# The last 2048 tokens through Strassen's scheme in two blocks, and the low parts of q, k and v on GpSimd

## The chip, the core and the metric

The kernel runs on one core of a Trainium2 chip. The metric is device time in microseconds (us) of one execution; before the change the median of three runs was 1136.08 us (1135.66 to 1136.82). The engines are called as in the profile: PE is TensorE (PEld its weight loads), DVE is VectorE, ACT is ScalarE, POOL is GpSimd, and SP is SyncE, whose queue issues nearly all DMAs.

## The reference

Causal attention with a decay of cumulated logarithms, for 8 batches of 8 heads, 576 tokens, 64 dimensions; then a feed-forward network (FFN) with softplus on all 4608 tokens:

```python
scores = np.matmul(q, k.transpose(0, 1, 3, 2)) / np.sqrt(D)
cum = np.cumsum(np.log(np.clip(f, 0.0001, 1.0)), axis=-1)
scores = np.where(causal, -1e9, scores + cum[:, :, :, None] - cum[:, :, None, :])
attn = softmax(scores, axis=-1)
x = np.matmul(attn, v)                     # tokens x 512 after the heads are joined
h = x @ w_in                               # 4608 x 512 @ 512 x 2048
g = np.maximum(h, 0.0) + np.log1p(np.exp(-np.abs(h)))
out = g @ w_out                            # 4608 x 2048 @ 2048 x 512
```

All is float32. The kernel keeps the precision by splitting a factor into a high and a low part of a narrower type (suffixes h and l) and multiplying three times: high by high, high by low, low by high.

## The kernel before

**Attention.** Batch 0 is treated apart, in plain float32. Batches 1 to 7 are 56 jobs of one head each. A job computes scores in six pieces (L859 and L860, 12 matmuls; the piece of 64 columns marks one job's start in a trace), the row minimum with the mask on DVE (L864), the exponential on ACT (L903), the division by the row sum (L933) on ACT, POOL or DVE, turns the weights on PE (L996, 15 short matmuls a job), splits them into ph and pl, multiplies with the split v (L1143, 10 matmuls), and adds two parts into x (L1193). So 37 PE instructions a job are attention.

**The operands of the scores.** q and k of a job lie in a tile T, of which there are two, used in turn: job n + 2 takes the tile of job n. `prepare` fills it when the last score of job n has been read: the high part (L227, T from raw), the low part `l_` (L811, on DVE), and four moves by DMA from one half of the partitions to the other (L814): one after the high part, one after the low part, one after that move, and one after both. The first score of job n + 2 waits for the last move. v has a high part and a low part `vl` (L785, on DVE).

**FFN.** Tokens 0 to 511 go in two plain blocks and one of 256; tokens 512 to 3583 in six wide blocks of 512. For each of 16 chunks of 128 of the 2048 middle columns, a wide block takes 12 matmuls of 512 columns up (L1336) and, for four tiles of 128 tokens, 12 down (L1423): 384 in a block. Between lies the gate, three passes on ACT (L1369, L1372, L1375), one on DVE (L1383), and the split of g (L1391). Half of a block's down products come at its end, as a tail, from parts of g kept in DRAM. A block starts when the attention of its last token is done, and its matmuls are dealt out among the steps of the following jobs.

**Strassen.** The last 1024 tokens (`super_block`, one of them) wait until all attention is issued. Even and odd tokens, two halves of the 512 inputs and pairs of chunks make 2 by 2 blocks; Winograd's form of Strassen's scheme takes seven products in place of eight. For each of eight pairs of chunks that is 7 x 6 matmuls up (L1856); down is as before, 12 for each chunk (L1978). POOL adds blocks of the weights (L1738), DVE adds products (L1885), and `lay_x` makes the sums of x (L1648) and splits them (L1678).

**The order.** Python lists all steps, and a planner with costs (`Plan.run`) sets each engine's order by when it expects a step's inputs and buffers to be there. Engines then run their lists and wait by semaphores. `on` in `add` names the engines that a step may go to, with a cost, a bias and a mark for steps that share a port of the memory.

Of the kernel before, what the change touches and what calls it, by code (L numbers as in the profile page):

```python
# [31 lines left out]
FFN_RANK = 0  # L32
SHORT = 512
SUPER, NSUPER = 1024, 1
BEHIND = 190
# [7 lines left out]
class Op:  # L43
# [4 lines left out]
    def __init__(self, on, emit, after, takes, lag):  # L48
        self.on = on if isinstance(on, list) else [on]
        self.emit, self.after, self.takes, self.lag = emit, list(after), takes, lag  # L50
        self.users = []
        self.missing = len(self.after)


class Plan:
# [33 lines left out]
    def start_of(self, op, clock):  # L89
# [4 lines left out]
        for tag in set(op.takes):  # L94
            n, free = op.takes.count(tag), self.free[tag]
            early = self.queue[tag][0] is not op
            if len(free) < n + early or (early and not op.loose):
                return None
# [132 lines left out]
def tile_decay_attention_softplus_ffn(  # L231
# [113 lines left out]
    g_d = dpool.tile([2, NFC, P, TB], F32, name="g_d")  # L345
    odd_d = dpool.tile([NSUPER, 2, NFC, P, SUPER // 2], F32, name="odd_d")
# [316 lines left out]
    def attention(job):  # L663
# [114 lines left out]
        def split_v():  # L778
# [11 lines left out]
            vl = add(subs(nv * D), v_lo, after=[vh])  # L790
# [3 lines left out]
        def prepare():  # L794
# [29 lines left out]
            l_ = add(On("DVE", 0.75, 0.0, True), lo, after=[h_])  # L824
# [8 lines left out]
        def stat_tile(ti, into=None):  # L833
# [12 lines left out]
            for i, (a, z, acc) in enumerate(pieces):  # L846
# [31 lines left out]
                else:  # L878
                    o = add(on, scores, after=st["T"], takes=("att",), loose=True)
                if quad:  # L880
# [340 lines left out]
    splits = {}  # L1221
# [29 lines left out]
    def ffn_block(i):  # L1251
# [11 lines left out]

        def split_x():
            if plain:
                st["split"] = [d for a, z, d, _ in wrote[0] if a < t0 + nt and z > t0]
                return
            ready, low, at = [], [], t0
            while at < t0 + nt:
# [25 lines left out]
                if lo + w == S:  # L1295
                    give("x32", splits[b])
                at += w
            st["split"], st["low"] = ready, low
# [249 lines left out]
    def super_blocks():  # L1548
# [66 lines left out]
        spots = [(x, j) for x in OPERANDS for j in range(2)]  # L1615
# [5 lines left out]
        def lay_x(t0):  # L1621

            done, reads, pieces = {}, {}, []
            pos = t0
            while pos < t0 + SUPER:
                b, lo = pos // S, pos % S
                w = min(t0 + SUPER - pos, S - lo)
                pieces.append((b, lo, w, slice((pos - t0) // 2, (pos - t0 + w) // 2)))
                pos += w

            WHERE = dict(B11=(0, 0), B12=(0, 1), B21=(2, 0), B22=(2, 1))

            for j in range(2):
                room = {}

                def less(x, one, other, j=j, room=room):

                    if x not in room:
                        box = {}

                        def begin(e, box=box):
                            box["x"] = buf("fe", [P, 512], f"late_{x}{t0}_{j}")

                        room[x] = box, add(NO_ENGINE, begin, takes=("fe",), lag=0.0), [], []
                    box, begun, made, _ = room[x]

                    def go(e, a, b, c):
                        e.tensor_sub(box["x"][:, c], a(), b())  # L1648

                    for i, (b, lo, w, c) in enumerate(pieces):  # L1650
                        (a1, n1), (a2, n2) = (value(v, i) for v in (one, other))
                        o = add(
                            [subs(w // 2), On("POOL", 0.2 + w * 0.0011, 0.0, True)], lambda e, a1=a1, a2=a2, c=c: go(e, a1, a2, c),
                            after=n1 + n2 + [begun],
                        )
                        made.append(o)
                        for v in (one, other):
                            (room[v][3] if v in room else reads.setdefault(b, [])).append(o)

                def value(x, i, j=j, room=room):  # L1660
# [532 lines left out]
    for n in range(len(jobs) + 1):  # L2193
# [56 lines left out]
        if n >= nstart:  # L2250
            while splits_left:
                splits_left.pop(0)()
# [54 lines left out]
```

## Time and profile before

| | |
|---|---|
| median of three runs | 1136.08 us |
| the profiled execution, its own time | 1137.25 us |
| its span, first to last instruction | 1135.4 us |
| TensorE clock granted over the span | 0.999 (2.4 GHz all the way) |
| busy share of PE, DVE, ACT, POOL | 99%, 75%, 74%, 16% |

The span falls into batch 0 and the weights (to about 114 us), the 56 jobs with the FFN between them (to 950 us), and Strassen's block with the last tails (to the end). PE counts as busy from an instruction's start to its modelled end, and these overlap; how fast it works is read from the distance of starts.

### The profile page before, as it was taken

Reading aid. Unit: us, or ns where it says so; the run is one execution under the profiler, and the core shown is the slowest. Engines: PE = TensorE matmul, PEld = TensorE weight load, DVE = VectorE, ACT = ScalarE, POOL = GpSimd, SP = SyncE. Lnnn points to the kernel's source line nnn. Section 1 sums busy time; section 2 is a strip of 40 time slices with the busy share of each in tenths; the row PEclk is TensorE's granted clock in tenths of the full one; section 3 lists DMA queues with packets and bytes.
Section 4 is the critical chain, followed back from the end, with each engine's and each line's share of the span. In section 5 each row is a group of like instructions: output and inputs, shape, how many; then the busy total and the mean of one; then the engine's idle time right before and its main releaser. Section 6 shows DMA issues by size and latency. Waiting matters only on the chain.

```text
span 1135.4 us, 19910 instructions
## 1 busy us (share of the span) xinstructions
PE 1123.0 (99%) x6230; PEld 939.8 (83%) x6230; DVE 850.8 (75%) x2131; ACT 838.8 (74%) x2033; POOL 185.6 (16%) x225
## 2 busy tenths in 40 slices
PE   9999999999999999999999999999999999999998
PEld 7766789888888888888888888888888888888887
DVE  7888999987787777777777778677867778867610
ACT  6888798889877777678767787677867875766610
POOL 3323221111111001000010000000000013555200
PEclk9999999999999999999999999999999999999999
DMA  8868676566575656666576466665657535322481
GB/s 244 252 183 229 179 215 163 148 174 175 158 208 159 174 164 175 161 186 170 151 203 189 137 179 182 165 179 158 174 153 208 142 99 162 130 93 98 162 278 38
DMA packets 160489, 192.97 MB, mean 170 GB/s; under 512 B 54944, under 2 KB 120768, under 8 KB 160384
## 3 DMA queue, kind: packets, MB, share of 16 engines
q1 hardware_dynamic: 160216, 191.55, 59.1%
q8 instruction: 50, 0.82, 0.3%
q14 instruction: 55, 0.45, 0.1%
q10 hardware_dynamic: 168, 0.15, 0.0%
HBM read 114.17 MB, written 44.34 MB: 140 GB/s over the span
## 4 chain that ended last, share of the span: by engine, by line
PE 86%; DVE 8%; ACT 3%; DMA 2%; issue 1%; SPq 0%; DVEq 0%
PE acc L1423 24%; PE h L1336 24%; PE b L996 7%; PE o L1143 7%; PE late_E L1978 4%; PE s L860 4%; PE s L859 4%; PE late_A L1856 2%; PE late_D L1856 2%; PE late_C L1856 2%; DVE s L864 1%; PE late_B L1856 1%; PE late_D L1978 1%; PE late_C L1978 1%; PE late_A L1978 1%
## 5 line engine op out<-in xcount | busy, mean ns | idle before, releaser
L864 DVE CUSTOM_DVE_ANT_0 s<-s,cmask 128x288 f32<-128x288 f32 (+6 forms) x320 | 137.1, 440 | 60.6 <-PE s L860 54.2
L903 ACT ACTIVATE pb<-s,negm 128x288 f32<-128x288 f32 (+5 forms) x272 | 143.3, 531 | 45.8 <-DVE negm L864 43.9
L933 POOL TENSOR_SCALAR pb<-pb,rsum 128x448 f32<-128x448 f32 (+2 forms) x44 | 59.5, 1353 | 415.8 <-ACT e L1375 192.9
L1336 PE MATMUL h<-xh,wl 128*128 128x512 f32 (+1 forms) x448 | 126.0, 380 | 0.0
L1336 PE MATMUL h<-xh,wih 128*128 128x512 f32 (+1 forms) x448 | 117.0, 383 | 0.5 <-DVE gl L1391 0.5
L1018 DVE TENSOR_TENSOR pl<-b,ph 128x512 fp32r<-128x512 f32 x168 | 107.1, 662 | 9.5 <-ACT ph L227 8.7
L1336 PE MATMUL h<-xl,wih 128*128 128x512 f32 (+1 forms) x448 | 113.9, 376 | 0.0
L227 ACT CAST ph<-b 128x512 fp32r<-128x512 f32 (+2 forms) x169 | 80.1, 492 | 34.8 <-PE b L996 33.1
L859 PE MATMUL s<-T 128*128 128x192 f32 (+1 forms) x336 | 99.3, 304 | 3.0 <-ACT pb L903 1.3
L1423 PE MATMUL acc<-woh_dt_float32r,gh 128*128 128x512 f32 x248 | 99.2, 400 | 0.0
L1369 ACT ACTIVATE e<-h 128x512 f32<-128x512 f32 x112 | 66.8, 596 | 43.3 <-PE h L1336 42.2
L860 PE MATMUL s<-T 68*128 68x192 f32 (+1 forms) x336 | 98.2, 296 | 0.0
L1423 PE MATMUL acc<-woh_dt_float32r,gl 128*128 128x512 f32 x248 | 97.4, 393 | 0.0
L1423 PE MATMUL acc<-wol_dt_float32r,gh 128*128 128x512 f32 x248 | 97.1, 392 | 0.0
L1336 PEld LDWEIGHTS h<-xl,wih 128*128 128x128 f32 x448 | 80.8, 188 | 16.6
L1336 PEld LDWEIGHTS h<-xh,wl 128*128 128x128 f32 x448 | 80.1, 189 | 13.0 <-issue 0.5
L1383 DVE SCALAR_TENSOR_TENSOR h<-h,e 128x512 f32<-128x512 f32 x104 | 73.3, 705 | 20.4 <-ACT e L1375 19.4
L1336 PEld LDWEIGHTS h<-xh,wih 128*128 128x128 f32 x448 | 77.8, 189 | 11.8 <-DVE gl L1391 0.7
L1143 PE MATMUL o<-ph,vhl 128*128 128x512 f32 x336 | 84.8, 290 | 0.0
L1391 DVE TENSOR_TENSOR gl<-h,gh 128x512 fp32r<-128x512 f32 x104 | 71.5, 687 | 16.0 <-ACT gh L227 14.6
L996 PE MATMUL b<-halves,pb 128*128 128x128 f32 x512 | 82.2, 272 | 0.0
L1372 ACT ACTIVATE e<-e 128x512 f32<-128x512 f32 x112 | 70.8, 632 | 1.9
(368 smaller groups left out, 2812.9 us busy)
## 6 DMA issues: line engine op xcount, KB each, us to landing
T<-T SPq DMA_DIRECT2D x224, 144.0 KB
wl<-wil_d SPq DMA_DIRECT2D x56, 512.0 KB
raw<-in_qkT SPq DMA_DIRECT2D x112, 144.0 KB
g_d<-gh SPq DMA_DIRECT2D x84, 128.0 KB
g_d<-gl SPq DMA_DIRECT2D x84, 128.0 KB
vr<-in_vR SPq DMA_DIRECT2D x64, 160.0 KB
out<-ob SPq DMA_DIRECT2D x28, 256.0 KB
sto<-in_w_out SPq DMA_DIRECT2D x11, 512.0 KB
```

Source lines behind the costliest of these rows:

```text
L227: (e.tensor_copy if hasattr(e, "tensor_copy") else e.copy)(out, in_)
L859: e.matmul(o, qA[:, S - end : S - q0], kA[:, a:z], start=True, stop=False)
L860: e.matmul(o, qB[0:ST, S - end : S - q0], kB[0:ST, a:z], start=False, stop=True)
L864: e.tensor_tensor_reduce(out=box["o"], in0=box["o"], in1=cmask[0:n_q, right - w : right], scale=-0.125, scalar=m0 if i else 3.0e38, op0=AL ...
L903: e.activation(o, box["o"], AF.Exp, bias=m1, scale=-1.0, accum_out=acc)
L996: e.transpose(box["ps"][0 : x.shape[1], at : at + one.shape[1]], x, one)
L1018: e.tensor_sub(box["l"], box["ps"][:, 0:w], box["h"].bitcast(F32))
L1143: e.matmul(boxes[gi]["ps"][0:m, a:z], st["vhl"][:, c, 0:m], pbox[which][:, o : o + z - a], start=gi in fresh and which == "h", stop=gi == ...
L1336: e.matmul(o, l, r, start=m == 0, stop=m == 11)
L1423: e.matmul(st["acc", tt], l, r[fc], start=first and m == 0, stop=last and m == 2,)
L1856: e.matmul(banks[to], stationary(x, j), at(b, y, j), start=start and m == 0, stop=m == 5, skip_group_check=not start,)
L1978: e.matmul(banks[x], l, r[fc], start=first and m == 0, stop=final and m == 2)
```

## The change

`NSUPER` goes from 1 to 2: tokens 2560 to 4607 go through Strassen's scheme, in two blocks of 1024, after all attention; wide blocks are left for tokens 512 to 2559, four in place of six. T still has two tiles.

x of batches 1 to 7 is written to a tensor `x_d` in DRAM, four DMAs of 288 KB a batch, each when two heads are done. The wide blocks behind token 1152 and both Strassen blocks load x from there (1 MB a load), where before they read the tile that attention had written; a tile of x is free once it is stored.

The low parts `vl` and `l_` may go to POOL, with a bias that prefers it by 9 us.

The pacing of the FFN among the jobs has new constants, and a rule that saves matmuls of a block for later jobs. The first Strassen block's second half of odd outputs is accumulated in the banks of the even ones (E0, E1) and reads through the buffers gh and gl; its last eight steps are issued behind the second block's start.

```diff
-SUPER, NSUPER = 1024, 1
-BEHIND = 190
+SUPER, NSUPER = 1024, 2
+POOLB = -9.0
+BEHIND, FILL, REST, START = 190, 5, 4, 3
...
-            vl = add(subs(nv * D), v_lo, after=[vh])
+            vl = add([subs(nv * D), On("POOL", 0.2 + nv * D * 0.0022, POOLB, True)], v_lo, after=[vh])
...
-            l_ = add(On("DVE", 0.75, 0.0, True), lo, after=[h_])
+            l_ = add([On("DVE", 0.75, 0.0, True), On("POOL", 0.2 + S * 0.0022, POOLB, True)], lo, after=[h_])
...
+    def store_x(b, g):
+
+        def store(e):
+            e.dma_start(out=x_d[g, :, b * S : (b + 1) * S], in_=x_of[b][:, g, :])
+
+        need = [d for _, _, d, g_ in wrote[b] if g_ == g]
+        stores[b, g] = add_dma(store, 288, after=need)
...
+        def split_stored():
+            ready, low, box = [], [], {}
+
+            def load(e):
+                box["x"] = buf("x32", [P, NCC, S], f"xr{i}")[:, :, 0:nt]
+                e.dma_start(out=box["x"], in_=x_d[:, :, t0 : t0 + nt].rearrange("c p t -> p c t"))
...
+            if t0 + nt > 2 * S:
+                split_stored()
+                return
...
+                ld = add_dma(load, 1024, after=stored(t0, SUPER, (j, j + 2)), takes=("x32",))
...
-            two = tail(["C", "D"], 2 * P, s == NSUPER - 1)
+            end = s == NSUPER - 1
+            spots = [(x, j) for x in OPERANDS[: 7 if end else 2] for j in range(2)]
+            one = tail(["B", "A"], 0, spots, False)
+            two = tail(["E0", "E1"], 2 * P, spots, end)
...
-        share = sum(c for c, _ in ffn) / (until - n + 1 + DELAY) / max(1, len(units))
+        here = sum(c for c, _ in ffn)
+        share = here / (until - n + 1 + (START if n <= nstart + H else DELAY))
+        if n > nstart + H:
+            later = sum(NFC * on_pe(WIDE, 24).cost for x in ready_at.values() for _ in x)
+            share = min(share, (here + later) / (len(jobs) - n + REST))
+        share /= max(1, len(units))
...
-        plan.late, left = 0, []
-        for unit in units:
+        plan.late, left = 0, units[len(units) - 8 :]
+        for unit in units[: len(units) - 8]:
             unit()
+    for unit in left:
+        unit()
```

**PE.** Between the last scores of one job (s_4_288) and the first of the next (s_1_0) in the steady part stood 24 FFN matmuls (h, acc) and the ten of the values (o). Before, at the 37th job, the first half of them:

```order
L859 MATMUL s_4_288_7812<-T_1151 128x288
L860 MATMUL s_4_288_7812<-T_1151 128x288
L1423 MATMUL acc_0_7676<-woh_dt_float32r,gh_3_7717 128x512
L1423 MATMUL acc_0_7676<-wol_dt_float32r,gh_3_7717 128x512
L1423 MATMUL acc_0_7676<-woh_dt_float32r,gl_3_7722 128x512
L1423 MATMUL acc_1_7677<-woh_dt_float32r,gh_3_7717 128x512
L1423 MATMUL acc_1_7677<-wol_dt_float32r,gh_3_7717 128x512
L1423 MATMUL acc_1_7677<-woh_dt_float32r,gl_3_7722 128x512
L1336 MATMUL h_6_7829<-xh_6951,wih 128x512 x4
L1336 MATMUL h_6_7829<-xh_6951,wl_3_7639 128x512 x2
L1143 MATMUL o_1_7842<-ph_1_7749,vhl_7314 128x512
L1143 MATMUL o_1_7842<-pl_1_7755,vhl_7314 128x512
```

In the changed kernel at the 38th job, one of the closest places (L866 and L867 are the scores, L1151 the values, L1479 the down products):

```order
L866 MATMUL s_4_288_7322<-T_1370 128x288
L867 MATMUL s_4_288_7322<-T_1370 128x288
L1151 MATMUL o_1_7328<-ph_1_7293,vhl_6925 128x512
L1151 MATMUL o_1_7328<-pl_1_7305,vhl_6925 128x512
L1479 MATMUL acc_0_7026<-woh_dt_float32r,gh_4_7184 128x512
L1479 MATMUL acc_0_7026<-wol_dt_float32r,gh_4_7184 128x512
L1479 MATMUL acc_0_7026<-woh_dt_float32r,gl_4_7194 128x512
L1479 MATMUL acc_1_7027<-woh_dt_float32r,gh_4_7184 128x512
L1479 MATMUL acc_1_7027<-wol_dt_float32r,gh_4_7184 128x512
L1479 MATMUL acc_1_7027<-woh_dt_float32r,gl_4_7194 128x512
L1151 MATMUL o_1_7328<-ph_2_7302,vhl_6925 128x448
L1151 MATMUL o_0_7349<-ph_0_7291,vhl_6925 128x64
```

Behind these come six more values and then the next job's first score: six FFN matmuls stand there, where before 24 stood. Over the 47 jobs from the ninth to the last but one the changed order has 1479 FFN matmuls of 512 columns, 31.5 a job, and the order before 2178, or 46.3 a job.

**POOL.** In the steady part, POOL had the division of some weights (pb or p by rsum) alone, one or two a job:

```order
L933 TENSOR_SCALAR pb_93<-pb_93,rsum_87 128x448
L933 TENSOR_SCALAR p_92<-p_92,rsum_88 64x64
L933 TENSOR_SCALAR pb_94<-pb_94,rsum_88 128x320
L933 TENSOR_SCALAR p_91<-p_91,rsum_89 64x64
L933 TENSOR_SCALAR pb_93<-pb_93,rsum_89 128x320
```

In the changed kernel each job has two more there, the low part of v (L792) and that of q and k (L818):

```order
L792 TENSOR_TENSOR vhl_5364<-vr_5234,vhl_5364 128x6x64
L818 TENSOR_TENSOR T_1370<-raw_5193,T_1370 128x576
L941 TENSOR_SCALAR p_92<-p_92,rsum_90 64x64
L792 TENSOR_TENSOR vhl_5493<-vr_5405,vhl_5493 128x6x64
L818 TENSOR_TENSOR T_1137<-raw_5350,T_1137 128x576
L941 TENSOR_SCALAR p_91<-p_91,rsum_87 64x64
L792 TENSOR_TENSOR vhl_5651<-vr_5575,vhl_5651 128x6x64
L818 TENSOR_TENSOR T_1370<-raw_5484,T_1370 128x576
```

All 56 low parts of q and k and all 56 of v have moved from DVE to POOL, and T's moves now follow a POOL instruction that stands behind the low part of v.

**SP.** Stores of x stand in the queue that issues T's moves. In the changed kernel, about the 36th job:

```order
L777 DMA raw_6940<-in_qkT 64x9x64
L781 DMA raw_6940<-in_qkT 64x576
L719 DMA vr_6954<-in_vR 128x320
L724 DMA vr_6954<-in_vR 128x1x64
L1234 DMA x_d<-x_5_6743 128x576
L821 DMA T_1137<-T_1137 64x576
L1363 DMA wl_3_6990<-wil_d 128x1024
```

The store (L1234) has come in ahead of the last move (L821) of a tile T; before, such places held loads and the stores of g and of the output.

## Rows read from the trace of the kernel before

**Rows 1.** The page: busy time and share of the span, the span in 40 slices for some engines and the granted clock, and the shares by engine of the chain that ended last.

```profile
PE 1123.0 (99%) x6230; PEld 939.8 (83%) x6230; DVE 850.8 (75%) x2131; ACT 838.8 (74%) x2033; POOL 185.6 (16%) x225
...
PE   9999999999999999999999999999999999999998
...
DVE  7888999987787777777777778677867778867610
ACT  6888798889877777678767787677867875766610
...
PEclk9999999999999999999999999999999999999999
...
PE 86%; DVE 8%; ACT 3%; DMA 2%; issue 1%; SPq 0%; DVEq 0%
```

**Rows 2.** Timeline of PE near the end: start and duration of single matmuls of 512 columns, the first and the last of 36 in a row.

```profile
1085.15 0.39 PE L1978 MATMUL late_B<-woh_dt_float32r,late_T 128*128 128x512 f32 x1
1085.37 0.39 PE L1978 MATMUL late_B<-wol_dt_float32r,late_T 128*128 128x512 f32 x1
...
1093.08 0.39 PE L1978 MATMUL late_A<-woh_dt_float32r,late_T 128*128 128x512 f32 x1
```

**Rows 3.** Busy time by stretch: from:to and length in us, then PE, PEld, DVE, ACT and POOL busy (with the number of instructions), the granted clock, the DMA share and GB/s. The first holds seven jobs, the ninth to the fifteenth; the second six jobs of the steady part; the third the first eight jobs; the fourth runs from the last values to Strassen's first product; the fifth lies in Strassen's block.

```profile
211.98:304.20 92.22, 91.75 (x518) 78.36 (x517) 73.06 (x192) 80.92 (x206) 11.22 (x11) 1.00 0.58 159
594.18:693.85 99.67, 99.67 (x540) 84.82 (x539) 75.95 (x190) 78.18 (x188) 6.16 (x5) 1.00 0.58 163
114.00:211.98 97.98, 97.05 (x655) 81.48 (x656) 93.94 (x256) 85.24 (x229) 19.74 (x18) 1.00 0.69 188
950.15:962.44 12.29, 12.29 (x55) 10.14 (x55) 12.14 (x30) 5.28 (x14) 4.33 (x6) 1.00 0.63 198
990.00:1079.00 89.00, 89.00 (x394) 73.74 (x393) 61.05 (x109) 58.73 (x110) 38.12 (x51) 1.00 0.36 125
```

**Rows 4.** Groups of equal instructions in the first stretch of rows 3: the wide FFN matmuls and the score piece of 64 columns, one a job.

```profile
L1336 PE MATMUL h<-xh,wl 128*128 128x512 f32 x56 | 16.6, 395 | 0.0
L1336 PE MATMUL h<-xh,wih 128*128 128x512 f32 x56 | 15.6, 401 | 0.5 <-DVE gl L1391 0.5
L1336 PE MATMUL h<-xl,wih 128*128 128x512 f32 x56 | 15.1, 392 | 0.0
L1423 PE MATMUL acc<-woh_dt_float32r,gl 128*128 128x512 f32 x33 | 12.9, 392 | 0.0
L1423 PE MATMUL acc<-woh_dt_float32r,gh 128*128 128x512 f32 x32 | 12.8, 401 | 0.0
L1423 PE MATMUL acc<-wol_dt_float32r,gh 128*128 128x512 f32 x32 | 12.5, 391 | 0.0
...
L859 PE MATMUL s<-T 128*64 128x64 f32 x7 | 1.3, 193 | 0.0
```

**Rows 5.** Groups over the whole span: the low parts of q and k (L811) and of v (L785) on DVE, and on POOL the division of weights (L933) and two-input sums of 256 columns (L1738); busy us, mean ns of one, idle before.

```profile
L811 DVE TENSOR_TENSOR T<-raw,T 128x576 fp32r<-128x576 f32 x56 | 42.3, 755 | 0.2
L785 DVE TENSOR_TENSOR vhl<-vr,vhl 128x384 fp32r<-128x384 f32 x56 | 31.7, 565 | 1.2 <-ACT vhl L227 0.6
...
L933 POOL TENSOR_SCALAR pb<-pb,rsum 128x320 f32<-128x320 f32 x18 | 21.3, 1183 | 145.4 <-DVE rsum L917 71.6 <-DVE x L1193 37.4 <-ACT x L227 19.0
...
L1738 POOL TENSOR_TENSOR p<-p,p 128x256 f32<-128x256 f32 x16 | 12.0, 747 | 1.3
...
L933 POOL TENSOR_SCALAR pb<-pb,rsum 128x576 f32<-128x576 f32 x4 | 6.9, 1722 | 0.0
```

**Rows 6.** Timeline of one tile T in the dense part: the last score of its job, the high and low parts, the moves (L814; the last line holds the fourth and others), and the first score of the job after next.

```profile
194.50 0.30 PE L860 MATMUL s<-T 68*128 68x288 f32 x1
...
194.77 0.45 DVE L227 CAST T<-raw 128x576 fp32r<-128x576 f32 x1
...
195.50 1.32 SPq L814 DMA_DIRECT2D T<-T  x2
195.57 0.75 DVE L811 TENSOR_TENSOR T<-raw,T 128x576 fp32r<-128x576 f32 x1
...
199.57 0.51 SPq L814 DMA_DIRECT2D T<-T  x1
...
202.73 2.37 SPq L814 DMA_DIRECT2D T<-T  x3
...
207.14 0.25 PE L859 MATMUL s<-T 128*128 128x192 f32 x1
```

**Rows 7.** Waits of SP's queue over the whole span, by line: us in total, times, longest us.

```profile
SPq L1395 <- ACT gh L227: 85.0, 38, 5.1
...
SPq L814 <- DMA T<-T: 53.9, 50, 3.5
```

**Rows 8.** Timeline of POOL and DVE about a low part of v.

```profile
825.39 0.44 POOL L933 TENSOR_SCALAR p<-p,rsum 64x64 f32<-64x64 f32 x1 [9.14 <-PE s L860]
...
825.88 0.86 DVE L785 TENSOR_TENSOR vhl<-vr,vhl 128x384 fp32r<-128x384 f32 x1
```

**Rows 9.** Timeline of PE at the longest single wait of the steady part, in brackets.

```profile
450.78 0.33 PE L859 MATMUL s<-T 128*128 128x192 f32 x1 [0.94 <-ACT ph L227]
```

More of the change, by code (lines that the diff above doesn't have):

```diff
@@ L51, in __init__ @@
         self.users = []
+        self.end = self.guard = None
         self.missing = len(self.after)
@@ L95, in start_of @@
             n, free = op.takes.count(tag), self.free[tag]
-            early = self.queue[tag][0] is not op
+            head = self.queue[tag][0]
+            early = 0 if head is op else head.takes.count(tag) if EARLY else 1
             if len(free) < n + early or (early and not op.loose):
+                return None
+            if early and op.guard and op.guard.end is None:
                 return None
@@ L1218, in attention, with stored @@
         )
-    splits = {}
+    splits, stores = {}, {}
+    def store_x(b, g):
[3 more added lines that the diff above has]
+        stores[b, g] = add_dma(store, 288, after=need)
+        if b > 1 and g == NCC - 1:
+            give("x32", [add(NO_ENGINE, mark, after=[stores[b, c]]) for c in range(NCC)])
+    def stored(t0, n, planes=range(NCC)):
+        return [stores[b, g] for b in range(t0 // S, (t0 + n - 1) // S + 1) for g in planes]
     kept_read = {}
@@ L1294, in split_x @@
                 splits.setdefault(b, []).append(l_)
-                if lo + w == S:
-                    give("x32", splits[b])
                 at += w
+                if b == 0 and lo + w == S:
+                    give("x32", splits[0])
+                if b == 1 and at == t0 + nt:
+                    give("x32", splits[1] + [add(NO_ENGINE, mark, after=[stores[1, g]]) for g in range(NCC)])
             st["split"], st["low"] = ready, low
@@ L1621, in lay_x @@
         def lay_x(t0):
[L1623 to L1631, printed above, removed]
-            for j in range(2):
[L1634 to L1660, printed above, removed]
-                    b, lo, w, c = pieces[i]
@@ new lines, in value, with less, go @@
+                    return (lambda: xbox["x"][:, k, odd:SUPER:2]), [ld]
+                def less(x, one, other, j=j, room=room, reads=reads, value=value):
+                    box = {}
+                    (a1, n1), (a2, n2) = value(one), value(other)
+                    def go(e):
+                        box["x"] = buf("fe", [P, 512], f"late_{x}{t0}_{j}")
+                        e.tensor_sub(box["x"], a1(), a2())
+                    o = add(
+                        [subs(n), On("POOL", 0.2 + n * 0.0022, 0.0, True)], go, after=n1 + n2,
+                        takes=("fe",), loose=True,
+                    )
+                    room[x] = box, None, [o], []
+                    for v in (one, other):
+                        (room[v][3] if v in room else reads).append(o)
@@ L1701, in lay_x @@
                     give("fe", ops)
-            for b, ops in reads.items():
-                give("x32", splits.get(b, []) + ops)
+                give("x32", reads)
             return done
@@ L2036, in step @@
                     loads["used", fp].append(o)
+                    if not spots_of[fp] and tiles[-1] == k == 1:
+                        give("gh", [o])
+                        give("gl", [o])
                     return o
```

114 lines of the change are left out of this document (75 added, 39 removed).

## The prediction

> **What bounds the kernel now.** I read the page first. PE is busy for 99% of the span at the full clock of 2.4 GHz, and the chain that ended last is 86% PE; in 39 of the 40 slices PE is at nine tenths or more [rows 1]. Busy time of PE says little, since starts overlap, so the second view is the distance of starts: near the end 36 matmuls of 512 columns start between 1085.15 and 1093.08 us, which is 7.93 / 35 = 0.2266 us for one [rows 2]. That is the price of one FFN matmul wherever PE has all it needs.
>
> The third view is the table by stretch [rows 3]. In the steady part six jobs take 99.67 us with 540 PE instructions. A job has 37 of attention, so 540 - 222 = 318 are FFN matmuls (some counted at the edges): 318 x 0.2266 = 72.1 us, and (99.67 - 72.1) / 6 = 4.6 us of PE are left for a job's attention, waits included. In the dense part seven jobs take 92.22 us with 168 + 97 = 265 FFN matmuls [rows 4]: 60.0 us, and (92.22 - 60.0) / 7 = 4.6 us again. So a job costs 4.6 us and 0.2266 us for each FFN matmul beside it, at either density. PE's own work is the bound, and the first question is how many matmuls the change takes away.
>
> **The change part by part.** *Fewer matmuls up.* Two wide blocks took 2 x 16 x 12 = 384 up; Strassen's block takes 8 x 7 x 6 = 336. Down stays 384. That is 48 x 0.2266 = 10.9 us off PE's list, at the price of a place where PE never waits.
>
> *720 matmuls leave the attention part.* They go to a stage where PE, in the stretch of rows 3 that lies there, is busy 89.00 of 89.00 us, with DVE at 69% and ACT at 66% [rows 3], and a second block of the same steps has the same loads. Nothing is lost there.
>
> *The 56 jobs stand closer.* The changed order has 31.5 FFN matmuls a job where 46.3 stood, so a job should take 4.6 + 31.5 x 0.2266 = 11.7 us, against 4.6 + 46.3 x 0.2266 = 15.1. Whether ACT and DVE keep up is the open question. ACT: 80.92 / 7 = 11.6 us a job in the dense part at 37.9 FFN matmuls, and 78.18 / 6 = 13.0 us in the steady part at 53 [rows 3]; the line through these has 0.10 us a matmul, and gives 10.9 us at 31.5. DVE the same way: 10.4 and 12.7 us, 0.15 a matmul, 9.5 us at 31.5; from that go the two low parts, 0.755 + 0.565 = 1.3 us [rows 5], which leaves 8.2. Together 19.1 us on two engines that have 23.4: 82%. The dense part had 22.0 of 26.3, or 83%, and steps that may go to either engine can even it out. So the nearest row for the coming density is the dense part, where PE was busy 91.75 of 92.22 us, and a job cost no more than elsewhere. I take 0.5% of 47 x 11.7 = 550 us, 2.8 us, as lost to waits. From below: none. From above, by the first eight jobs, with DVE at 96%: 97.98 - 97.05 is 1% [rows 3], 5.5 us; and one wait of 0.94 us, the longest of the steady part [rows 9], shows what a single miss costs.
>
> *Low parts on POOL.* A two-input sum of 256 columns takes 0.747 us there; between 320 and 576 columns a division grows by 1.722 - 1.183 = 0.54 us, so 2.1 ns a column [rows 5]. Estimates from these: 1.4 us for 576 columns and 1.0 us for 384 (by plain proportion 1.7 and 1.1). POOL had 11.22 / 7 = 1.6 us a job in the dense part [rows 3], so some 4 of 11.7 us: far from full. DVE is relieved; but the low part of q and k is a link in T's cycle, which grows by 1.4 - 0.755 = 0.65 us. That costs nothing as long as T is ready before PE has run out of other work. In the dense part a cycle took 207.14 - 194.50 = 12.6 us from the last score to the first score of the job after next [rows 6], so 13.3 with POOL. Counted in the changed order, with the distances that the same instructions had before, PE has 13.4 us of work at the shortest between those two scores, 15.9 on the mean. So the cover is there, thin in some five jobs: 0 us, and 0.65 in each if it is gone, 3 us.
>
> The Trainium skill speaks against this move: GPSIMD Engine Reference, section 4.1, gives elementwise work to VectorE, GpSimd being about twice as slow for two inputs. The rows agree, 1.4 against 0.755 us; the sum would change only through the cycle of T, which is the last rival below. SBUF — State Buffer, section "Who interferes with whom", adds that a GpSimd instruction and a DVE instruction with two SBUF inputs shut each other out for a whole instruction. One row agrees: a low part of v that began while POOL worked took 0.86 us in place of 0.565 [rows 8].
>
> What is left on DVE of that kind is little once the low parts are gone; at 0.3 us for each of two POOL steps a job DVE would go from 8.2 to 8.8 us of 11.7. PE would not see it.
>
> *x through DRAM.* Four stores of 288 KB a batch in SP's queue, and seven loads of 1 MB. No row shows these; the nearest are the moves of T, 144 KB, whose landings SP waited for 50 times, 3.5 us at most [rows 7]. Before a block's first products that adds a store and a load, perhaps 10 us. The changed order keeps a wide block's tail, over 60 matmuls, for two jobs there, some 23 us of PE work, so I cost it at nothing; uncovered, three times 5 us. A store that waits in SP's queue holds back the moves of T behind it; waits of one kind there reach 5.1 us already [rows 7]. This too would come out as a longer cycle of T.
>
> *The joints.* Before, 54 matmuls covered the way from the last values to the first Strassen product, 12.29 us without a gap [rows 3]; now 66 do. Between the blocks the changed order mixes the last steps of one with the first products of the other. 0 us, at most 2. *The start* (to 114 us) is ordered anew in small ways: 0, with 3 us to either side; DVE, at 96% in the first eight jobs, is relieved there, which could give 2 us back.
>
> **Sum.** Span 1135.4 - 10.9 + 2.8 + 0 = 1127.3 us. The median of the runs was 0.7 us above the profiled span (1136.08 against 1135.4): 1128.0 us.
>
> **The rivals.** *All of the gain and more.* No added waits, and DVE's relief tells in the first jobs, where PE lost 0.93 us to plain idling [rows 3] and more to matmuls that started late: 1136.1 - 10.9 - 2 to 3 = 1122 to 1123. For it: ACT and DVE together are no fuller than in the dense part. Against it: more jobs have it tight at once.
>
> *ACT becomes the bound of the attention part.* At 10.9 of 11.7 us a job, before anything moves from it, ACT is at 93%; exponentials and gates queue behind one another, scores wait for banks, and each job takes 0.23 us more. 47 x 0.23 = 10.8 us: no change, 1136. For it: ACT was at 88% in the dense part and 78% in the steady one. Against it: PE did not notice the 88%.
>
> *T's cycle becomes the bound; slower.* Two tiles serve jobs in turn, so two periods have to hold one cycle and the time a job spends between its first and last score. With 15.9 us of mean distance and a period of 11.7 that time is 2 x 11.7 - 15.9 = 7.5 us; the period is then (cycle + 7.5) / 2. At 13.3 us it would be 10.4, no bound; it passes 11.7 at a cycle of 15.9, and eats the whole gain at 11.7 + 10.9 / 47 = 11.93, a cycle of 16.4. Moves queued behind stores of x, and POOL's step behind two others, would have to add 3 us to rows 6. At a cycle of 17 the period is 12.25 and 47 x 0.55 = 26 us are lost: 1136.1 - 10.9 + 26 = 1151. For it: SP's queue waits in order, and the way is three moves long. Against it: 12.6 us was reached with the same queue.
>
> That the change doesn't do what it says is no rival: all 112 low parts stand in POOL's list, and the 48 matmuls are gone from PE's.
>
> **How the numbers follow.** Forecast as summed, with its own range 1123 to 1133: 0.66. All and more: 0.12. ACT bound, about 1136: 0.12. T bound: 0.10. The range reaches from 1121 to 1138; it leaves out most of the last case and the outer edge of the second. About 0.2%, 2.3 us, is what a measurement of this kernel can tell from no change. Faster by more than that (below 1133.8): 0.66 + 0.12 = 0.78; within it: 0.12; slower: 0.10.
>
> **What would show it.** Right: PE has 48 matmuls fewer; the 47 jobs take some 550 us; starts in both Strassen blocks lie 0.2266 us apart; the first score on a tile T comes when PE gets to it, without a wait, and low parts take 1.4 and 1.0 us on POOL. Wrong, if scores wait for T's moves or for banks in many jobs (a job then costs clearly over 4.6 us besides its FFN matmuls), if a wide block or a Strassen block waits for its load of x, or if the first 114 us differ by more than 3.

## The result, and the profile after

| | runs | median us | lowest to highest | profiled execution: time, span |
|---|---|---|---|---|
| before | 4 | 1136.22 | 1135.66 to 1136.82 | 1137.25, 1135.4 |
| after | 4 | 1145.11 | 1144.03 to 1149.47 | 1144.82, 1143.0 |

The ratio of the means is 1.0085, 95% interval 1.0059 to 1.0112. By the medians the change is 8.9 us slower, where 8 us faster was forecast, and outside the range.

The page of the changed kernel: busy time, the span in 40 slices for two engines, and the shares by engine of the chain that ended last. It answers to [rows 1].

```profile
PE 1123.4 (98%) x6188; PEld 935.7 (82%) x6188; DVE 834.3 (73%) x2076; ACT 859.9 (75%) x2087; POOL 363.5 (32%) x402
...
PE   9989999999999999999999999999999999999998
...
ACT  6778888888987889878989778896577753666610
...
PE 57%; ACT 5%; DVE 3%; issue 1%; DVEq 0%; ACTq 0%
```

PE has fewer matmuls and is as busy as it was, in a longer span. That is the first sign: a matmul that starts late counts as busy, so the loss does not show as idle time on the page. ACT stands at 8 and 9 tenths in many of the slices that hold the close jobs.

Next the table by stretch, the kernel before ahead of the one after; the columns are those of [rows 3]. The four stretches are cut at the first score of the first, the ninth and the 56th job.

```profile
0.00:113.99 113.99, 108.35 (x736) 82.30 (x737) 96.41 (x263) 88.94 (x212) 41.00 (x68) 1.00 0.79 228
113.99:211.99 98.00, 97.07 (x655) 81.50 (x656) 93.96 (x256) 85.26 (x229) 19.74 (x18) 1.00 0.69 188
211.99:926.75 714.76, 712.78 (x3913) 606.57 (x3912) 540.54 (x1385) 557.11 (x1382) 59.69 (x54) 1.00 0.61 168
926.75:1135.44 208.69, 204.80 (x929) 169.39 (x927) 119.91 (x229) 107.44 (x213) 65.14 (x85) 1.00 0.41 136
```

```profile
0.00:115.62 115.62, 109.11 (x740) 84.05 (x741) 98.89 (x271) 89.24 (x211) 39.99 (x66) 0.99 0.76 226
115.62:212.33 96.71, 93.39 (x618) 79.17 (x617) 82.44 (x224) 81.76 (x221) 34.02 (x29) 0.98 0.69 184
212.33:782.28 569.95, 563.73 (x3238) 477.42 (x3236) 445.48 (x1224) 491.14 (x1287) 163.08 (x146) 1.00 0.69 191
782.28:1143.03 360.75, 357.21 (x1598) 295.08 (x1596) 207.44 (x360) 197.78 (x370) 126.40 (x162) 1.00 0.45 148
```

Times of stretches alone say nothing here, since matmuls moved between them. From each I take off its FFN and Strassen matmuls at 0.2266 us for 512 columns (half for 256 columns, four times as much per column for the few FP32 ones of the start). What is left is attention's own PE time and everything that went wrong:

| stretch | before | after | loss |
|---|---|---|---|
| to the ninth job | 212.0 us | 212.3 us with 24 matmuls of 256 and 12 of 512 columns fewer (5.4 us) | +5.8 |
| the 47 jobs | 714.8 - 493.5 = 221.2, or 4.71 a job (2178 FFN matmuls) | 569.9 - 335.1 = 234.8, or 5.00 a job (1491) | +13.6 |
| the rest | 208.7 - 870 x 0.2266 = 11.6 | 360.7 - 1545 x 0.2266 = 10.6 | -1.0 |
| 48 matmuls fewer | | | -10.9 |

The sum is 7.5 us, and the spans differ by 1143.0 - 1135.4 = 7.6. So the gain came as forecast (the FFN and Strassen matmuls of the traces are 48 fewer), the two Strassen blocks cost nothing, and two stretches took back more than the gain: the 47 close jobs, and the start.

In the close jobs these are PE's waits as the view of waits lists them, with the releaser; columns: us in total, times, longest. First before, then after.

```profile
PE s L859 <- ACT ph L227: 0.9, 1, 0.9
PE b L996 <- ACT pb L903: 0.6, 1, 0.6
PE h L1336 <- DVE gl L1391: 0.5, 1, 0.5
```

```profile
PE h L1392 <- DVE gl L1447: 1.7, 3, 1.0
PE s L866 <- ACT p L911: 1.0, 3, 0.6
PE s L866 <- DVE pl L1026: 0.7, 2, 0.4
PE h L1392 <- ACT xh L233: 0.5, 1, 0.5
...
PE h L1392 <- DVE xh L233: 0.2, 1, 0.2
```

Three kinds have become nine, with no large one: a gate that ends late (gl), an exponential that holds a bank (p), a weight's low part (pl), and the halves of x that came through DRAM (0.7 us). No wait names a move of T. The waits grew from 2.0 to 5.4 us; most of the 13.6 us is in delays too short for this view. Taking for each PE instruction the distance to the next start (of FFN matmuls what is over 0.2266 us), by kind over the 47 jobs:

| | scores | transposes | values | FFN over 0.2266 | sum |
|---|---|---|---|---|---|
| before | 76.0 | 62.3 | 69.7 | 13.3 | 221.2 |
| after | 82.5 | 64.4 | 73.3 | 14.6 | 234.8 |

The low parts on POOL (idle before, last column, costs POOL nothing):

```profile
L818 POOL TENSOR_TENSOR T<-raw,T 128x576 fp32r<-128x576 f32 x46 | 65.9, 1434 | 301.0 <-ACT T L233 146.1 <-DVE T L233 71.8 <-issue 48.8
L792 POOL TENSOR_TENSOR vhl<-vr,vhl 128x384 fp32r<-128x384 f32 x46 | 46.9, 1020 | 41.8 <-DVE vhl L233 20.2 <-ACT vhl L233 11.1 <-DMA T<-T 3.3
```

1.43 and 1.02 us stand where 1.4 and 1.0 were estimated.

In the start one place stands out. The same two stretches, before and then after:

```profile
60.00:72.00 12.00, 11.34 (x76) 8.46 (x78) 10.44 (x28) 9.88 (x22) 2.33 (x3) 1.00 0.73 215
72.00:80.00 8.00, 7.85 (x60) 6.30 (x56) 7.63 (x20) 7.61 (x18) 2.94 (x3) 1.00 0.75 209
```

```profile
60.00:72.00 12.00, 7.58 (x52) 4.92 (x51) 11.74 (x31) 10.62 (x25) 5.04 (x6) 0.99 0.80 266
72.00:80.00 8.00, 8.00 (x37) 6.06 (x37) 5.22 (x12) 5.52 (x13) 1.86 (x3) 0.80 0.36 116
```

PE is idle for 4.4 of 12 us, and then the granted clock stands at its lower level, 1.2 GHz, for 3.41 us (the mean over the second stretch is 0.80). The clock falls once more at 181.09 us, after 5.09 us in which PE was busy for 3.71. Two times 3.41 us at half clock cost at most 3.4 of the start's 5.8 us.

### The profile page after: what moved, and what is told of

It is laid out like the page before. It is cut to its first block, busy times and chain, and to the rows that moved or that the text cites. A ratio compares the mean times of both kernels' runs of the same rounds, so it can differ in the third digit from the quotient of the medians.

```text
span 1143.0 us, 20131 instructions
## 1 busy us (share of the span) xinstructions
PE 1123.4 (98%) x6188; PEld 935.7 (82%) x6188; DVE 834.3 (73%) x2076; ACT 859.9 (75%) x2087; POOL 363.5 (32%) x402
## 4 chain that ended last, share of the span: by engine, by line
PE 57%; ACT 5%; DVE 3%; issue 1%; DVEq 0%; ACTq 0%
PE late_E L2025 11%; PE acc L1479 10%; PE h L1392 8%; PE late_A L1904 4%; PE late_D L1904 4%; PE late_C L1904 4%; PE o L1151 4%; PE b L1004 3%; PE late_A L2025 2%; PE late_B L2025 2%; PE late_B L1904 2%; PE s L866 2%; PE s L867 2%; ACT pb L911 1%; ACT pb L939 1%
## 5 line engine op out<-in xcount | busy, mean ns | idle before, releaser
L818 POOL TENSOR_TENSOR T<-raw,T 128x576 fp32r<-128x576 f32 x56 | 80.6, 1440 | 340.5 <-ACT T L233 177.9
L866 PE MATMUL s<-T 128*128 128x192 f32 (+1 forms) x336 | 101.5, 311 | 4.5 <-ACT p L911 2.1
L867 PE MATMUL s<-T 68*128 68x192 f32 (+1 forms) x336 | 97.6, 296 | 0.0
L1392 PE MATMUL h<-xh,wl 128*128 128x512 f32 (+1 forms) x320 | 93.2, 378 | 0.0
L1151 PE MATMUL o<-ph,vhl 128*128 128x512 f32 x336 | 86.8, 295 | 0.3 <-DVE pl L1026 0.3
L1392 PE MATMUL h<-xh,wih 128*128 128x512 f32 (+1 forms) x320 | 82.8, 381 | 2.7 <-DVE gl L1447 1.9
L2025 PE MATMUL late_E<-woh_dt_float32r,late_g 128*128 128x512 f32 x256 | 82.6, 389 | 0.0
L1392 PE MATMUL h<-xl,wih 128*128 128x512 f32 (+1 forms) x320 | 79.9, 372 | 0.0
L939 ACT ACTIVATE pb<-pb,rsum 128x320 f32<-128x320 f32 (+2 forms) x128 | 77.4, 657 | 0.2
L792 POOL TENSOR_TENSOR vhl<-vr,vhl 128x384 fp32r<-128x384 f32 x56 | 57.4, 1025 | 55.7 <-DVE vhl L233 25.6
L866 PEld LDWEIGHTS s<-T 128*128 128x128 f32 (+1 forms) x336 | 60.6, 180 | 17.3 <-ACT p L911 4.1
L1479 PE MATMUL acc<-woh_dt_float32r,gh 128*128 128x512 f32 x176 | 70.6, 401 | 0.3 <-ACT gh L233 0.3
L1151 PEld LDWEIGHTS o<-ph,vhl 128*128 128x128 f32 x336 | 63.4, 189 | 8.5 <-issue 0.8
L1479 PE MATMUL acc<-woh_dt_float32r,gl 128*128 128x512 f32 x176 | 69.4, 394 | 0.0
L1479 PE MATMUL acc<-wol_dt_float32r,gh 128*128 128x512 f32 x176 | 69.0, 392 | 0.0
L867 PEld LDWEIGHTS s<-T 68*128 68x128 f32 (+1 forms) x336 | 60.6, 180 | 9.2 <-issue 1.4
```

The lines of the kernel that those rows point to most:

```text
L866: e.matmul(o, qA[:, S - end : S - q0], kA[:, a:z], start=True, stop=False)
L867: e.matmul(o, qB[0:ST, S - end : S - q0], kB[0:ST, a:z], start=False, stop=True)
L939: e.activation(a, a, AF.Copy, scale=f_)
L1151: e.matmul(boxes[gi]["ps"][0:m, a:z], st["vhl"][:, c, 0:m], pbox[which][:, o : o + z - a], start=gi in fresh and which == "h", stop=gi == ...
L1392: e.matmul(o, l, r, start=m == 0, stop=m == 11)
L1479: e.matmul(st["acc", tt], l, r[fc], start=first and m == 0, stop=last and m == 2,)
```

## The experiments

Theory A: with 31.7 in place of 46.3 FFN matmuls beside a job, PE has too little work of its own between the steps of attention and gates that depend on one another over ACT, DVE and POOL; they come late, in many small pieces. Theory B: it is the move of the low parts to POOL. Other theories: ACT alone as the bound; x through DRAM; T's cycle; the pace of the start.

All runs in one table. "Besides" is the time of one of the 47 jobs besides its FFN matmuls, as above; "half" is the time at half clock ahead of the last matmuls. Both are of the profiled execution. But for e8_start2 (all 13.7 us) and e4_no_log (3.4 us), the time at half clock lies ahead of the ninth job, so that "besides" is free of it.

| run | median us (runs) | ratio to before, 95% | span | ninth job at | FFN matmuls in 47 jobs | besides | half, us |
|---|---|---|---|---|---|---|---|
| before | | | 1135.4 | 212.0 | 2178 | 4.71 | 0 |
| after | 1145.11 (4) | 1.0085, 1.0059 to 1.0112 | 1143.0 | 212.3 | 1491 | 5.00 | 6.8 |
| e1_low_dve | 1152.93 (4) | 1.0134, 1.0103 to 1.0165 | 1152.8 | 214.6 | 1500 | 5.13 | 13.7 |
| e3_before_low_pool | 1135.05 (10) | 0.9981, 0.9972 to 0.9991 | 1134.1 | 207.2 | 2202 | 4.70 | 0 |
| e4_no_log | 1155.42 (4) | 1.0154, 1.0122 to 1.0186 | 1153.9 | 218.2 | 1488 | 5.05 | 23.9 |
| e5_one_block | 1153.82 (4) | 1.0142, 1.0119 to 1.0164 | 1153.1 | 210.4 | 2214 | 4.95 | 3.4 |
| e6_act_less | 1140.21 (10) | 1.0026, 1.0012 to 1.0039 | 1134.8 | 207.5 | 1491 | 4.91 | 0 |
| e7_dve_less | 1136.95 (10) | 1.0007, 0.9993 to 1.0021 | 1134.7 | 209.3 | 1491 | 4.86 | 6.8 |
| e8_start2 | 1145.33 (4) | 1.0073, 1.0058 to 1.0088 | 1143.0 | 210.3 | 1455 | 5.13 | 13.7 |
| e9_both_less | 1136.72 (10) | 1.0005, 0.9991 to 1.0020 | 1133.2 | 208.8 | 1491 | 4.86 | 6.8 |
| e10_pace_scales_free | 1135.46 (12) | 0.9988, 0.9977 to 1.0000 | 1132.2 | 207.6 | 1470 | 4.96 | 0 |
| e11_pace_scales_dve | 1145.04 (6) | 1.0074, 1.0054 to 1.0094 | 1139.3 | 206.5 | 1470 | 5.06 | 0 |
| e12_padded | 1190.45 (4) | 1.0478, 1.0454 to 1.0501 | 1187.6 | 208.5 | 1747 | 4.77 | 0 |
| e13_chain_less | 1134.43 (10) | 0.9983, 0.9969 to 0.9997 | 1136.5 | 212.4 | 1491 | 4.83 | 10.2 |

**Low parts back on DVE, in the changed kernel.**

```diff
-POOLB = -9.0
+POOLB = 99.0
```

> The changed kernel with the low parts of q, k and v back on DVE; two Strassen blocks, closer jobs and x through DRAM stay. Theory A (closeness: with 31.5 in place of 46.3 FFN matmuls beside a job, ACT and the chain score - exponential - weights no longer keep up, and PE loses some 0.4 us more a job, whoever makes the low parts): 1142 to 1149 us, as the changed kernel, since DVE had room. Theory B (the slower step on POOL delays T and v and so the scores): the loss of 47 x 0.4 = 19 us goes, 1124 to 1131 us.

1152.93 us. Theory B expected 1124 to 1131 and falls; A's 1142 to 1149 was too low. The jobs cost 5.13, more than with POOL, and the start has 13.7 us at half clock. The planner made a new order for this run.

**Low parts on POOL, in the kernel before.**

```diff
-            vl = add(subs(nv * D), v_lo, after=[vh])
+            vl = add(On("POOL", 0.2 + nv * D * 0.0022, -9.0, True), v_lo, after=[vh])
...
-            l_ = add(On("DVE", 0.75, 0.0, True), lo, after=[h_])
+            l_ = add(On("POOL", 0.2 + S * 0.0022, -9.0, True), lo, after=[h_])
```

> The kernel before with one edit: all low parts of q, k and v on POOL. Theory A: 1135 to 1138 us, no change, as PE has 46 FFN matmuls a job to wait behind. Theory B: 47 x 0.2 to 0.4 us more, 1145 to 1155 us.

1135.05 us, ratio 0.9981: the jobs are unchanged at 4.70, and the kernel is faster by 0.2%. B is out from both sides. The rule of the Trainium skill that the prediction weighed (GPSIMD Engine Reference, section 4.1: elementwise work belongs on VectorE) holds for the single step, 1.43 us against 0.755 [rows 5]; for this kernel the slower engine was the better place, since nobody waited for it.

**No logarithm, planned anew.**

```diff
-            a = add(on_act(512), log, after=[a])
+            if plain:
+                a = add(on_act(512), log, after=[a])
```

> The changed kernel without the logarithm pass in the gates of the wide blocks (exp(-|x|) is used in the place of log(1 + exp(-|x|)) there; the Strassen blocks keep theirs). That is 0.63 us less on ACT for each of 65 gates in the stretch, 0.9 us a job. Theory A with ACT as what is short: PE gets back most of the 19 us, 1126 to 1134 us. A with another link (DVE's minima, banks) as what is short: 1140 to 1145 us. Theory B: 1140 us or more.

1155.42 us, with less work on ACT. By its letter this speaks against A. But the planner, which now counted without the pass, wrote another order for every engine, and the profile has 23.9 us at half clock (at most 12 us lost). An experiment that lets the order change tells of the order. The cuts below therefore take work out where it is issued and leave the plan's costs alone, so that each instruction keeps its place.

**One Strassen block.**

```diff
-SUPER, NSUPER = 1024, 2
+SUPER, NSUPER = 1024, 1
...
-BEHIND, FILL, REST, START = 190, 5, 4, 3
+BEHIND, FILL, REST, START = 190, 5, 2, 3
```

> The changed kernel with one Strassen block in place of two (six wide blocks, some 46 FFN matmuls beside a job again; the pace's REST 2 in place of 4, so that the plan closes); low parts on POOL, x through DRAM, the new pace of the start stay. Theory A (closeness costs 0.23 us a job, 10.9 us): the 48 matmuls saved and these 10.9 us both go, and what the start loses (8 us) stays: 1140 to 1145 us; the jobs at 4.7 us besides their FFN matmuls. If the jobs stay at 4.9 us, something else of the change, x through DRAM or SP's queue, is what they pay for: 1150 us or more.

1153.82 us; A expected 1140 to 1145 and missed, and the other case came, 1150 or more. At 47.1 FFN matmuls a job the jobs still cost 4.95, 11.5 us over the kernel before in all. The waits differ in kind:

```profile
PE h L1392 <- ACT xh L233: 4.1, 3, 2.7
PE acc L1479 <- DMA gh_5b<-g_d: 1.4, 1, 1.4
PE s L866 <- DVE x L1201: 0.8, 1, 0.8
```

The longest of them in its timeline, the load of x from DRAM, its high part, and PE behind it:

```profile
458.73 0.38 SPq L1291 DMA_DIRECT2D xr<-x_d  x1
467.60 1.04 ACT L233 CAST xh<-xr 128x1024 fp32r<-128x1024 f32 x1 [1.99 <-DMA xr<-x_d]
...
468.70 1.20 PE L1392 MATMUL h<-xh,wih 128*128 128x512 f32 x4 [2.72 <-ACT xh L233]
```

The load takes 8.9 us, and where the order has less than that to give, PE waits. In the changed kernel the same kind of wait is 0.7 us (above). Job by job the loss lies elsewhere than in the changed kernel: the median job costs 4.66 us here, 4.63 in the kernel before and 4.88 in the changed one, and the one job that waits for this load takes 10.1 and so holds some 5.5 of the 11.5 us. So with the density back the usual job is cheap again, as A has it, and this run has a loss of its own in a few places; by its sum it does not decide on closeness.

**Less work on ACT, on DVE, on both; the order kept.** The logarithm pass is not issued, or the sum after it is done for 64 columns, or both:

```diff
             def log(e):
-                e.activation(box["e"], box["e"], AF.Ln, bias=1.0)
+                if plain:
+                    e.activation(box["e"], box["e"], AF.Ln, bias=1.0)
...
-                e.scalar_tensor_tensor(h, h, 0.0, box["e"], ALU.max, ALU.add)
+                h = h[:, 0:64]
+                e.scalar_tensor_tensor(h, h, 0.0, box["e"][:, 0:64], ALU.max, ALU.add)
```

> The changed kernel with every instruction in its place on every engine, but the logarithm pass of the wide and the 256-token blocks' gates not issued (the gate is max(h, 0) + exp(-|h|) there): 0.63 us less on ACT for each gate, some 41 us in the 47 jobs. If ACT is what is late in these jobs: two thirds or more of PE's 15.6 us of waits over 0.1 us go, 1133 to 1138 us. If DVE is what is late: 1142 to 1146 us.

> The changed kernel with every instruction in its place, but the sum max(h, 0) + log(...) on DVE done for 64 of 512 columns in the wide and the 256-token blocks' gates: 0.57 us less on DVE for each gate, some 37 us in the 47 jobs, about as much as the run without the logarithm takes off ACT. If ACT is what is late: 1140 to 1146 us. If DVE is what is late: 1133 to 1138 us. If either engine relieves the chain alike, both runs gain about 5 us.

> The changed kernel with every instruction in its place, and both cuts of the two runs before together: no logarithm pass on ACT, and the sum after it on DVE for 64 of 512 columns, in the wide and the 256-token blocks' gates. Theory now: in the close jobs ACT and DVE share one chain (score, minimum, exponential, scale, high and low part; and the gates in the same queues), and what PE loses is that chain's lateness, not one engine's load. Then the two gains add: jobs at 4.75 us or less besides their FFN matmuls, 1127 to 1133 us. If one cut already took what there was, and the rest lies in the order itself or in the clock: 1134 to 1138 us.

What the two cuts take out, in the 47 jobs: the logarithm and the sum in the changed kernel, and the sum in e7_dve_less.

```profile
L1431 ACT ACTIVATE e<-e 128x512 f32<-128x512 f32 x66 | 41.7, 631 | 1.0
L1439 DVE SCALAR_TENSOR_TENSOR h<-h,e 128x512 f32<-128x512 f32 x66 | 46.3, 702 | 28.8 <-ACT e L1431 28.4
L1440 DVE SCALAR_TENSOR_TENSOR h<-h,e 128x64 f32<-128x64 f32 x66 | 15.6, 236 | 30.8 <-ACT e L1431 30.5
```

So 41.7 us go from ACT, and 46.3 - 15.6 = 30.7 from DVE, where 37 were expected.

The times are 1140.21, 1136.95 and 1136.72 us. The first lies between its two cases, the second in that of a late DVE. In the 47 jobs ACT's cut gives back 234.8 - 230.5 = 4.3 us, DVE's 6.2, both 6.6. ACT is not the bound: the cut on DVE is the smaller one and gives more, and the two do not add. Nor is DVE alone: with its cut 7.4 of the 13.6 us are left. The run with both cuts came out at the 1134 to 1138 us of its second case, not at 1127 to 1133. The runs of one kernel also differ: the ten of e6_act_less reach from 1135.74 us at a mean granted clock of 1.000 to 1142.50 at 0.997. A clock lower by 0.003 makes at most 0.003 x 1140 = 3.4 us, so the clock is up to half of that difference; the 47 jobs are therefore compared in profiles that have no half clock there.

**The pace of the start.**

```diff
-BEHIND, FILL, REST, START = 190, 5, 4, 3
+BEHIND, FILL, REST, START = 190, 5, 4, 2
```

> The changed kernel with the pace of FFN work in the first eight jobs as before (a divisor with 2 in place of 3, so more FFN matmuls early). If the pace is what costs the start its 8.5 us: 1137 to 1141 us, and job 8 begins with more FFN matmuls behind it. If it is the clock (two stretches of 3.41 us at half clock in the start) or the chain of the first jobs: 1143 to 1148 us.

1145.33 us, inside the 1143 to 1148 of its second case: no gain in the sum, but the start is mended. The first job begins at 111.3 us (115.6 with 3) and the ninth at 210.3, with all 424 FFN matmuls behind it, as before, and no half clock ahead of it. The gain goes in the 47 jobs, most plainly at the first wide block. PE, and then the same place by stretch:

```profile
230.72 0.30 PE L867 MATMUL s<-T 68*128 68x288 f32 x1
234.31 2.08 PE L1392 MATMUL h<-xh,wih 128*128 128x512 f32 x4 [3.29 <-DVE gl L1447]
```

```profile
225.00:231.00 6.00, 5.85 (x32) 4.79 (x30) 4.53 (x15) 5.56 (x17) 3.49 (x3) 1.00 0.67 154
231.00:234.30 3.30, 0.01 (x1) 0.00 (x0) 2.08 (x3) 3.30 (x8) 0.00 (x0) 0.84 0.65 204
233.27:240.10 6.83, 5.79 (x17) 4.54 (x18) 2.98 (x7) 3.18 (x9) 0.00 (x0) 0.50 0.53 177
```

A gate ends late, while ACT is busy for all of the 3.30 us; PE stands still for 3.29 us, and from 233.27 us on it has half the clock for 6.83 us. The Trainium skill tells of such gaps (TensorE: Matmul & The Clock Gate, section "HAM oscillation — how this bites in real kernels"): a wait that leaves PE idle is paid a second time, in the work behind it. This row agrees: 3.3 us of waiting, and up to 3.4 us more. A second stretch of 6.83 us at half clock begins at 342.50 us, so the clock can be up to 6.8 of these jobs' 241.2 us (besides their FFN matmuls); without that they would cost about the changed kernel's 234.8.

**Two other orders of the same work.**

```diff
-        On("DVE", 0.11 + n / 1920, SCALE_BIAS), on_act(n, 0.09), On("POOL", 0.24 + n * 0.0026),
+        On("DVE", 0.11 + n / 1920, SCALE_BIAS), on_act(n, 0.09), On("POOL", 0.24 + n * 0.0026, -0.3),
...
-POOLB = -9.0
+POOLB = -0.5
```

with START 2, and, as the second, START 2.25 with SCALE_BIAS 0.3 in place of 1.0 and nothing else.

> The changed kernel with three numbers of the planner changed: the pace of the first jobs as before (START 2), POOL preferred for the scaling of weights by 0.3 us, and the low parts of q, k and v on POOL only where that ends less than 0.5 us later than on DVE. Theory: the start's 5.3 us come back (as in the run with START 2), and what goes off ACT and DVE shortens the chain in the close jobs without the long wait at the first wide block that START 2 alone had: 1131 to 1137 us, level with the kernel before or below it. If close jobs lose some 13 us whatever the order: 1140 to 1146 us.

> The changed kernel with two numbers of the planner changed: START 2.25 in place of 3, and DVE's handicap for the scaling of weights 0.3 us in place of 1.0, so that scalings move from ACT to DVE, which has more room since the low parts left it. Theory (ACT and DVE share the lateness; start paced too thin): 1131 to 1138 us. If close jobs lose some 13 us whatever the order: 1140 to 1146 us.

1135.46 us, inside its 1131 to 1137, and 1145.04, outside its 1131 to 1138. Both mend the start (the first job begins at 111.2 and 110.8 us), neither has half clock in its profile, and the 47 jobs stay at 4.96 and 5.06. The first is level with the kernel before (0.9977 to 1.0000) and faster than the changed one; the second is as slow as that. What beats both kernels is e3_before_low_pool, the low parts on POOL alone, at 0.9981.

**More PE work, the order kept.** This is the test that e5_one_block did not give.

```diff
                     e.matmul(o, l, r, start=m == 0, stop=m == 11)
+                    if wide and m % 6 in (1, 3):
+                        e.matmul(o, l, r, start=False, stop=False)
```

> The changed kernel with every instruction in its place and two more matmuls of 512 columns in each half of a wide block's product up (the second and the fourth product of the half are added twice): 4 x 16 x 2 x 2 = 256 matmuls, 256 x 0.2266 = 58.0 us of PE work, all but the first few in the 47 jobs, which so have some 37 FFN matmuls each in place of 31.7. If what PE loses there is lateness of the attention's and the gates' chain, the added work lies in the gaps first: the time rises by some 46 to 51 us, to 1190 to 1196 us, and a job besides its FFN matmuls falls from 5.0 to 4.75 us or so. If the 13.6 us are a cost of PE's own (more switches between kinds of matmul, x through DRAM): the full 58 us, 1201 to 1205 us.

1190.45 us: 45.3 us more for 58.0 us of added matmuls. In the profile all 256 lie in the 47 jobs:

```profile
208.52:825.62 617.10, 614.62 (x3494) 525.68 (x3492) 449.27 (x1224) 495.59 (x1287) 162.45 (x146) 1.00 0.63 177
```

These take 617.1 in place of 569.9 us, 47.2 more, so 10.8 us of the added work lay in gaps. (The start is 3.8 us shorter, without half clock, which is why the whole grew by less.) A job costs 4.77 besides its FFN matmuls. By kind, scores take 76.3 (82.5 in the changed kernel, 76.0 before), transposes 62.9, values 71.7, FFN 13.1. So the added matmuls cost their full 0.2266 us, and what shrank is mostly the time of the scores. PE's waits are down to four:

```profile
PE h L1392 <- DVE gl L1449: 1.5, 2, 1.2
PE acc L1481 <- ACT gh L233: 0.3, 1, 0.3
PE o L1151 <- DVE pl L1026: 0.3, 1, 0.3
PE h L1392 <- DVE xh L233: 0.2, 1, 0.2
```

Same attention, same engines for each step, same order; only PE has more to do between. x through DRAM and the low parts on POOL are as in the changed kernel too. That shows the main point of theory A: of the 13.6 us at least 10.8 are lateness that more work on PE covers, and not a cost of PE's own. On which link the lateness arises it does not show, since more PE work gives time to ACT, DVE, POOL and the DMAs alike.

**The scalings left out too.** The two cuts in the gates, and the scaling function returns at once.

```diff
                 def scale(e, ti=ti, n_q=n_q, pi=pi, po=po):
-                    a, f_ = pt[pi][0:n_q, po : po + ends[ti]], rs[0:n_q, ti : ti + 1]
...
+                    return
```

> The changed kernel with every instruction in its place, both cuts in the gates as before (no logarithm pass, the sum for 64 of 512 columns), and the attention weights not scaled by the reciprocal of their row sums (five scalings a job not issued on ACT, DVE and POOL). If the rest of the loss (7 us after both cuts) is the attention's own chain on these engines: the jobs fall to 4.75 us or less besides their FFN matmuls, 1127 to 1133 us. If it is not on these engines (T's moves, order, PE itself): 1135 to 1138 us as with both cuts.

1134.43 us, between the two expectations. In the jobs 227.1 us are left, 7.7 fewer than in the changed kernel, and a wait that no other run had on top stands first:

```profile
PE s L866 <- DMA T<-T: 2.6, 2, 1.3
PE h L1388 <- DVE gl L1445: 0.6, 2, 0.3
```

Two waits for T's moves: perhaps the next link, once the others are shortened.

## Why the prediction was wrong

*Matmuls, joints, Strassen: right.* -10.9 us came; the rest after the 47 jobs lost nothing (-1.0).

*Low parts on POOL: right in size and in cost.* 1.43 and 1.02 us; no PE wait on T in the 47 jobs; e3_before_low_pool shows a small gain. The reading of [rows 8] was too strong: the POOL line shown there ended at 825.83 us, before the low part began. The POOL step beside the low part ran from 825.80 to 826.88, and DVE ended within it, at 826.74: it was slower, but not shut out.

*x through DRAM at nothing: right here, by the order's grace.* 0.7 us of waits; 4.1 us in e5_one_block, whose order gave the load less room.

*The 56 jobs stand closer, "lost to waits 2.8 us, 5.5 at most": the step that failed.* It measured 13.6 us. The step judged by busy shares: ACT and DVE together 82%, no fuller than in the dense part of [rows 3], so no worse. The shares came as forecast: 445.48 and 491.14 us of 569.95, 82% together (9.5 us a job on DVE where 8.2 was worked out, 10.4 on ACT where 10.9 was). The loss came all the same, so busy shares are not what gave out. e12_padded leaves ACT's and DVE's work as it is and brings the loss back to 2.8 us; taking 41.7 us off ACT or 30.7 off DVE brings back a third to a half. What gave out is PE's own work between dependent steps. Between a job's score of 288 columns and the next job's of 192 the traces have, before, 12 FFN matmuls at 22 of 41 places and 24 at 13; after, six at 12 of 27 places and 12 at 10. So 24 against six, as the change was described, is wider than the usual difference. The nearest row was also not near enough: the dense stretch had 37.9 FFN matmuls a job and cost 4.6, e12_padded has 37.2 and costs 4.77, and 31.7 cost 5.00. And the upper end, 1%, was PE's plain idle time in the first eight jobs [rows 3]. In the changed kernel's jobs that is 569.95 - 563.73 = 6.2 us, near the bound, against 2.0 before; the other 9.4 of the 13.6 us are starts that came late while PE counts as busy.

*The rival "ACT becomes the bound" came near in size and was wrong in cause.* It priced 0.23 us a job; the profile has 0.29 more than before. But ACT's cut alone brings back 4.3 of 13.6 us. *The T rival* did not come: in the changed kernel PE waited for T once, 0.7 us in the start, and never in the 47 jobs.

*The start, "0, with 3 us to either side": the second term that failed,* with 5.8 us. Two things make it up. The pace (START 3): 5.4 us of FFN work was moved out of a stretch that gets little shorter by it. With all 424 matmuls e8_start2 has its ninth job at 210.3 us, with 36 fewer e12_padded has it at 208.5, both without half clock ahead of it. And the clock: up to there e12_padded has the changed kernel's order, whose profile, with two stretches at half clock, has the ninth job 3.8 us later. Every run with START 3 has a gap of 1.5 to 2.4 us on PE at 67 to 72 us, and no run with 2 or 2.25 has it; in six of those nine profiles the clock fell at this gap. Each run with START 2 or 2.25 begins its first job at 110.8 to 111.3 us, those with 3 at 112.1 to 119.0. That pace was in the diff, and its price could have been read from the counts: 36 FFN matmuls fewer ahead of the ninth job.

What stays open: which link of the chain to shorten, since cuts on ACT and DVE do not add and all of them together (e13_chain_less) give back 7.7 of 13.6 us; and how much of any order's time is the order's own, since two settings of the planner with the same work lie 10 us apart.

## What to carry to other kernels

Before taking work away from the engine that bounds a kernel, ask what that work was covering: filler matmuls between dependent steps give other engines time, and taking them away there gains less than they cost. Here 10.8 of the 58.0 us of added matmuls cost nothing. Busy shares did not tell this; the amount of independent work between a step and its user does, and adding useless work with the order kept measures it: what does not show in the time was gap. To test one engine's load in a planned order, take the work out at the place where it is issued, and leave the plan alone.

## What was not expected of the hardware

Within the jobs FFN matmuls of 512 columns start 0.233 us apart on the mean before the change and 0.236 after it, not 0.2266 as in the Strassen blocks (0.2267 there in both). The first one behind a transpose has 0.31 us to the next start on the median, in both kernels.

The clock can cost as much as the gap ahead of it: in e8_start2 3.29 us without a matmul were followed by 6.83 us at half clock, and e4_no_log had 23.9 us at half clock in four places.
